# Attention products as 64x64 quarters of the array, with scores and values in one pair of banks

## The chip, the cores and the metric

The kernel runs on one core of a Trainium2 chip. The core has a matrix engine (TensorE, in the profile PE, with its weight loads as PEld), VectorE (DVE), ScalarE (ACT), GpSimd (POOL) and a queue engine (SP, SyncE) that issues the transfers here. Each engine works through a fixed list of instructions in order; semaphores make one wait for another. The metric is the time of one execution on the device in microseconds (us), lower is better.

## The reference

Two parts follow each other: attention within chunks of 64 tokens, then a feed-forward layer with a rational activation.

```
q, k, v: (8, 8, 576, 64)                       # batch, heads, tokens, head width; 9 chunks of 64 tokens
scores = matmul(q_c, k_c^T) / 8                # 64x64 for each chunk and head
attn = exp(scores - max); attn = attn / (sum(attn) + 1e-9)
x = matmul(attn, v_c)                          # back to (4608 tokens, 512)
h = x @ w_in                                   # (512, 2048)
P = a0 + a1*h + a2*h^2 + a3*h^3;  Q = 1 + |b0||h| + |b1|h^2
out = (P / (Q + 1e-6)) @ w_out                 # (2048, 512)
```

## The kernel before

The 4608 tokens are 36 units of 128 tokens: a unit is two chunks of 64 tokens with all eight heads. Three units make a block of 384 tokens, so there are 12 blocks. A block's feed-forward part has 8 steps, each over 256 of the 2048 inner columns.

**Feed-forward.** Each factor of the two large products is split into a high and a low part in the fp32r format, and three of the four partial products are summed. A step's first product is `ff1_mm`: 24 matmuls with 384 columns (line 252) into the tile `ph`, two banks of PSUM, of which there is one buffer. ScalarE copies it to `h` (line 281, one buffer too), then forms A, B and C (lines 282 to 284), a logarithm and an exponential (lines 288 and 289); VectorE makes `ghi` and `glo` of these (lines 293 to 306). The second product, `ff2_mm`, has 18 matmuls of 512 columns (line 334) into the three banks `po`. It is written two steps behind the first one (LAG).

**Attention of a unit** runs ahead, in the steps of the block before. `att_s` (line 163) makes the scores. Queries, keys and values lie with the two chunks in the upper and lower 64 partitions, and head pair (`hp`), head of the pair and 64 columns along the free side. The keys are kept in a tile `kbd` of twice the width, in which each chunk's rows have their keys on their own side and zeros on the other; so one matmul with 128 rows, 64 stationary columns (one head) and 128 moving columns gives both chunks' scores without mixing them. There are 8 of these, and they write the lower or upper 64 partitions of a bank, by head. Then come VectorE's maximum (line 183), eight exponentials of 64 columns with their sums on ScalarE (line 187), and the division. `att_t` (line 200) transposes the result on TensorE into the bank `pst` and copies it in two halves into `abd`, zero-padded like `kbd`. `att_av` (line 212) multiplies with the values, again 8 matmuls of the same shape, into the bank `psx`; ScalarE copies to `xhi`, and VectorE makes `xlo`.

**Banks.** PSUM has 8 banks: two for `ph`, three for `po`, and one each for `pss` (scores), `pst` and `psx`. The first three units' scores use `po`. Zeros are written once: by GpSimd into `abd`, into `kbd`, and into early keys of units 1 and 2, which borrow other tiles.

**Weights** arrive as float64 in 32 pieces of 512 columns. `piece_decode` (line 118) rewrites each with three instructions of VectorE and two of ScalarE; the low part is made by VectorE, or, for the pieces in LO_ON_PE, by two matmuls (lines 130 and 131) into a tile `pl`, which takes one of `pss`, `pst`, `psx` in turn. Four raw buffers hold the pieces in flight. PROLOGUE gives the order at the start, DECODED the pieces that are due before each of the first ten steps.

**What sets the order.** The instructions of all engines come from a scheduler, which takes the written order as priority and its own estimate of times. So a piece of a product can be put between others, and the order of the main loop is a wish only. The last two steps are written out by hand.

Of the kernel before, what the change touches and what calls it, by code (L numbers as in the profile page):

```python
# [29 lines left out]
KLN = 32  # L30
EXP_WIDE = (0, 1)
XLO_ON_PE = ()
LO_ON_PE = (7, 10, 11, 12, 13, 14, 16, 17, 18, 19, 20, 21, 22, 23, 25, 29)
PROLOGUE = "L0 L1 l1 L2 p1 l2 S0 S1 l1 V0 T0 p1 A0 p1 T1 p1 S2 V1 V2 A1 L3 T2 A2"
DECODED = (10, 11, 12, 16, 18, 25, 26, 28, 31, 32)
# [3 lines left out]
def tile_chunked_attention_rational_moe(  # L39
# [11 lines left out]
    nc = tc.nc  # L51
# [7 lines left out]

# [1 line left out]
    wi_hi = cp.tile([P, NHP, DFF], F32R, tag="wi_hi", name="wi_hi")  # L61
# [33 lines left out]
    def zero_rest(kt):  # L95
        nc.gpsimd.memset(kt[0:64, 1, :], 0.0)
        nc.gpsimd.memset(kt[64:128, 0, :], 0.0)

    def load_early(u):
        flat = lambda t: t.rearrange("p a b -> p (a b)")  # L100
        kt = p2.tile([P, NHP, BT], F32, tag=("xhi", "xlo")[u % 2], name=f"kt{u}")
        kt = flat(kt)[:, :1024].rearrange("p (a b) -> p a b", a=2)
        qt = p2.tile([P, 2, BT], F32, tag="A", name=f"qt{u}")
        vt = p2.tile([P, 2, BT], F32, tag="B", name=f"vt{u}")
        zero_rest(kt)
        load(u, flat(qt)[:, :512], kt, flat(vt)[:, :512], "q")
# [11 lines left out]
    def piece_decode(i, hi, lo):  # L118
# [8 lines left out]
        if i in LO_ON_PE:  # L127
            tag = ("pss", "pst", "psx")[i % 3]
            pl = ps_a.tile([P, 512], F32, tag=tag, name="pl")
            nc.tensor.matmul(pl, ident, val, start=True, stop=False)  # L130
# [28 lines left out]

# [1 line left out]
    ebuf = {}  # L161

    def att_s(u):
        qt, kt, vt = loaded[u]
        if u < UPB:
            pss = ps_o.tile([P, 512], F32, tag=f"po{u}", name=f"pss{u}")
        else:
            pss = ps_a.tile([P, 512], F32, tag="pss", name=f"pss{u}")
        for hp in range(NHP):
            for j in range(2):  # L170
                c0 = hp * 128 + j * 64
                nc.tensor.matmul(  # L172
                    pss[j * 64:(j + 1) * 64, hp * 128:(hp + 1) * 128],
                    qt[:, c0:c0 + 64],
                    kt[:, :, c0:c0 + 64],
                    start=True, stop=True,
                )
        g3 = pss.rearrange("p (g k) -> p g k", k=64)
        st = p2.tile([P, 4, 8], F32, tag="sm", name=f"sm{u}")
        mx, nm, sm, rs = (st[:, i, :] for i in range(4))  # L180
        e = p2.tile([P, 512], F32, tag="e", name=f"e{u}")
        e3 = e.rearrange("p (g k) -> p g k", k=64)
        nc.vector.tensor_reduce(mx, g3, AX.X, ALU.max)
        if EXP_ACCUM[u % 3] and u not in EXP_WIDE:
            nc.vector.tensor_scalar_mul(nm, mx, -0.125)
            for g in range(8):
                nc.scalar.activation(  # L187
                    e3[:, g, :], g3[:, g, :], AF.Exp,
                    bias=nm[:, g:g + 1], scale=0.125, accum_out=sm[:, g:g + 1],
                )  # L190
        else:
            nc.vector.tensor_sub(e3, g3, mx.unsqueeze(2).to_broadcast([P, 8, 64]))
            nc.scalar.activation(e, e, AF.Exp, scale=0.125)
            nc.vector.tensor_reduce(sm, e3, AX.X, ALU.add)
        nc.vector.tensor_scalar_add(rs, sm, 1e-9)
        nc.vector.reciprocal(rs, rs)
        nc.vector.tensor_mul(e3, e3, rs.unsqueeze(2).to_broadcast([P, 8, 64]))
        ebuf[u] = e

    def att_t(u):  # L200
        e = ebuf.pop(u)
        pst = ps_a.tile([P, 512], F32, tag="pst", name=f"pst{u}")
        for hp in range(NHP):
            c = slice(hp * 128, (hp + 1) * 128)
            nc.tensor.transpose(pst[:, c], e[:, c], ident)  # L205
        for par in range(2):
            rows = slice(64 * par, 64 * par + 64)
            nc.scalar.copy(abd[rows, par, :], pst[rows, :])

    xbuf = {}  # L210

    def att_av(u):
# [7 lines left out]
        qt, kt, vt = loaded.pop(u)  # L220
        psx = ps_a.tile([P, NHP, 128], F32, tag="psx", name=f"psx{u}")
        on_pe = u in XLO_ON_PE
        for hp in range(NHP):
            for j in range(2):
                c0 = hp * 128 + j * 64
                nc.tensor.matmul(  # L226
                    psx[j * 64:(j + 1) * 64, hp, :],
                    vt[:, c0:c0 + 64],
                    abd[:, :, c0:c0 + 64],
                    start=True, stop=not on_pe,  # L230
                )
        tk = slice(i * 128, (i + 1) * 128)
        nc.scalar.copy(xhi[:, :, tk], psx)
        if on_pe:
            nc.tensor.matmul(psx, nident, xhi[:, :, tk], start=False, stop=True)
            nc.scalar.copy(xlo[:, :, tk], psx)
        else:
            nc.vector.tensor_sub(xlo[:, :, tk], psx, xhi[:, :, tk].bitcast(F32))  # L238

# [1 line left out]
    gbuf = {}  # L241
# [112 lines left out]

# [1 line left out]
    win = lambda fq: [w_in_piece(fq, cc) for cc in range(NHP)]  # L356
# [29 lines left out]

# [1 line left out]
    total = RUN_NB * NST  # L388
    for g in range(total - 2):
# [8 lines left out]
        if n + 1 < RUN_NB and s % 2 == 0:  # L398
            if 0 < s // 2 <= UPB:
                att_av(u - 1)  # L400
                load(u)
            if s // 2 < UPB:
                att_s(u)
        if g >= LAG:
            n2, s2 = divmod(g - LAG, NST)
            ff2_mm(n2, s2)
            if s2 == NST - 1:
                store(n2)
        if n + 1 < RUN_NB and s % 2 == 1 and s // 2 < UPB:
            att_t(u)  # L410

# [1 line left out]
    with tc.manual_schedule():  # L413
# [57 lines left out]
```

## Time and profile before

| what | us |
|---|---|
| time, median of 3 runs (lowest to highest) | 972.9 (972.42 to 973.03) |
| the profiled execution, from its first to its last instruction | 971.9 |
| L252, first matrix: three groups of 760 matmuls, 260.0 + 256.9 + 256.6 | 773.5 |
| L334, second matrix: three groups of 570 matmuls, 227.3 + 222.8 + 150.4 | 600.5 |
| L172, scores: 544 + 32 records, 50.2 + 3.9 | 54.1 |
| L226, values: 576 records | 43.0 |
| L205, transposes: 144 | 22.8 |
| L187, exponentials: 272 of 128x64, mean 323 ns, with sums read behind each, mean 216 ns | 82.0 + 58.8 |
| L208, copies into abd: 72 of 64x512, mean 583 ns | 41.9 |

The times of groups add up to more than the engine's busy time, since a matmul's record goes on after the next one has begun. The profile names a group by line, engine, operation and tiles. Its chain of work that ended last follows back from the last instruction what each waited for. Its windows give busy times for chosen stretches, its timeline the instructions in order, where x16 is a number of records. The profiler lists no other time of the profiled execution than the span; the granted clock of TensorE was 0.993 on average.

### The profile page before, as it was taken

What the parts mean: (1) busy time and instruction counts of PE and PEld (TensorE: products, weight loads), DVE (VectorE), ACT (ScalarE), POOL (GpSimd) and SP (SyncE); (2) the same over time, 40 slices, a digit from 0 to 9 for tenths busy, and PEclk for the clock granted to TensorE, in tenths of its full rate; (3) what the DMA queues carried; (4) which work ended last, traced back from release to release, by engine and by line L of the source; (5) the groups of instructions that cost most, each with busy time, mean ns of one, the idle gap of its engine ahead of it and who ended that gap; (6) DMA issues with size and microseconds to landing.
All of it is one profiled execution on the core that took longest, in us unless ns stands there. A gap on an engine that the chain in (4) does not pass through costs nothing.

```text
span 971.9 us, 14009 instructions
## 1 busy us (share of the span) xinstructions
PE 942.6 (97%) x5376; PEld 816.3 (84%) x5376; DVE 787.5 (81%) x1011; ACT 702.0 (72%) x1353; POOL 4.9 (1%) x16
## 2 busy tenths in 40 slices
PE   4599999999999999999999999999999999999998
PEld 3477788898888888888888888888888888888996
DVE  6799999878787887887887887877877878877786
ACT  4799889758667777667767767775876776775764
POOL 2000000000000000000000000000000000000000
PEclk9799999999999999999999999999999999999999
DMA  7644423002002112101101100110111211100000
GB/s 252 189 154 142 163 87 110 12 1 66 4 30 66 33 33 65 34 12 59 61 12 52 56 24 26 62 44 23 65 33 34 65 33 34 65 12 1 33 1 33
DMA packets 26274, 55.43 MB, mean 57 GB/s; under 512 B 3680, under 2 KB 3680, under 8 KB 26208
## 3 DMA queue, kind: packets, MB, share of 16 engines
q1 hardware_dynamic: 26208, 54.54, 17.7%
q8 instruction: 42, 0.69, 0.3%
q14 instruction: 24, 0.20, 0.1%
HBM read 45.09 MB, written 9.44 MB: 56 GB/s over the span
## 4 chain that ended last, share of the span: by engine, by line
PE 89%; DVE 4%; DMA 3%; ACT 3%; issue 1%; SPq 1%; DVEq 0%; ACTq 0%
PE po L334 40%; PE ph L252 39%; PE pss L172 4%; PE psx L226 3%; DMA raw<-in_w_in 2%; PE pst L205 1%; DMA raw<-in_w_out 1%; PE pl L130 1%; ACT e L187 1%; DVE raw L124 1%; ACT raw L123 0%; DVE raw L125 0%; DVE raw L122 0%; SPq L90 0%; DVE C L295 0%
## 5 line engine op out<-in xcount | busy, mean ns | idle before, releaser
L252 PE MATMUL ph<-xhi,wi_hi 128*128 128x384 f32 x760 | 260.0, 342 | 3.7 <-ACT h L281 3.0
L252 PE MATMUL ph<-xlo,wi_hi 128*128 128x384 f32 x760 | 256.9, 338 | 0.2 <-DVE xlo L238 0.2
L252 PE MATMUL ph<-xhi,wi_lo 128*128 128x384 f32 x760 | 256.6, 338 | 0.0
L334 PE MATMUL po<-wo_hi,ghi 128*128 128x512 f32 x570 | 227.3, 404 | 0.0
L334 PE MATMUL po<-wo_lo,ghi 128*128 128x512 f32 x570 | 222.8, 396 | 0.0
L281 ACT COPY h<-ph 128x768 f32<-128x768 f32 x95 | 76.1, 802 | 202.1 <-PE ph L252 199.3
L252 PEld LDWEIGHTS ph<-xhi,wi_hi 128*128 128x128 f32 x760 | 143.3, 189 | 14.1 <-ACT h L281 4.4
L293 DVE SCALAR_TENSOR_TENSOR B<-B,ab,A 128x768 f32<-128x768 f32 x95 | 96.6, 1017 | 67.7 <-ACT B L283 67.1
L334 PE MATMUL po<-wo_hi,glo 128*128 128x512 f32 x570 | 150.4, 397 | 0.0
L252 PEld LDWEIGHTS ph<-xlo,wi_hi 128*128 128x128 f32 x760 | 143.4, 189 | 3.9 <-DVE xlo L238 0.7
L252 PEld LDWEIGHTS ph<-xhi,wi_lo 128*128 128x128 f32 x760 | 143.4, 189 | 0.8 <-issue 0.5
L334 PEld LDWEIGHTS po<-wo_hi,ghi 128*128 128x128 f32 x570 | 107.0, 188 | 27.0 <-issue 5.3
L303 DVE SCALAR_TENSOR_TENSOR ghi<-C,ab,A 128x768 fp32r<-128x768 f32 x94 | 95.7, 1018 | 41.7 <-ACT A L289 35.6
L334 PEld LDWEIGHTS po<-wo_hi,glo 128*128 128x128 f32 x570 | 106.7, 188 | 26.3 <-issue 0.8
L334 PEld LDWEIGHTS po<-wo_lo,ghi 128*128 128x128 f32 x570 | 107.0, 188 | 21.5 <-issue 1.6
L288 ACT ACTIVATE A<-B,cst 128x768 f32<-128x768 f32 x95 | 89.6, 943 | 13.4 <-DVE B L293 13.0
L305 DVE SCALAR_TENSOR_TENSOR B<-C,ab,B 128x768 f32<-128x768 f32 x95 | 96.8, 1019 | 2.5
L295 DVE SCALAR_TENSOR_TENSOR C<-C,ab,h 128x768 f32<-128x768 f32 x95 | 96.6, 1017 | 1.9
L284 ACT ACTIVATE C<-h,ab 128x768 f32<-128x768 f32 x95 | 96.6, 1017 | 0.1
L306 DVE TENSOR_TENSOR glo<-B,A 128x768 fp32r<-128x768 f32 x94 | 89.9, 956 | 5.4
L294 DVE TENSOR_TENSOR C<-C,h 128x768 f32<-128x768 f32 x95 | 90.4, 952 | 3.8 <-ACT C L284 3.8
L304 DVE SCALAR_TENSOR_TENSOR B<-B,ghi 128x768 f32<-128x768 f32 x94 | 90.0, 957 | 2.5
(95 smaller groups left out, 993.4 us busy)
## 6 DMA issues: line engine op xcount, KB each, us to landing
qt<-in_qT SPq DMA_DIRECT2D x36, 256.0 KB, 2.9
vt<-in_vP SPq DMA_DIRECT2D x36, 256.0 KB, 2.8
out<-o SPq DMA_DIRECT2D x36, 256.0 KB, 2.2
kbd<-in_kT SPq DMA_DIRECT2D x68, 128.0 KB, 3.3
raw<-in_w_in SPq DMA_DIRECT2D x16, 512.0 KB, 4.8
raw<-in_w_out SPq DMA_DIRECT2D x16, 512.0 KB, 3.7
kt<-in_kT SPq DMA_DIRECT2D x4, 128.0 KB, 4.7
ab<-in_a SPq DMA_DIRECT2D x1, 2.0 KB, 2.5
```

Source lines behind the costliest of these rows:

```text
L252: nc.tensor.matmul(acc, w, x[:, cc, :], start=(k == 0), stop=(k == 11))
L281: yield nc.scalar.copy(h, ph[:, :, :BT])
L284: yield nc.scalar.activation(C, h, AF.Identity, bias=a2, scale=a3)
L288: nc.scalar.activation(A, B, AF.Ln, bias=cst[:, 0:1], scale=2.0 ** -KLN)
L293: yield nc.vector.scalar_tensor_tensor(B, B, b1a, A, ALU.mult, ALU.add)
L294: yield nc.vector.tensor_mul(C, C, h)
L295: yield nc.vector.scalar_tensor_tensor(C, C, a1, h, ALU.add, ALU.mult)
L303: yield nc.vector.scalar_tensor_tensor(ghi, C, a0, A, ALU.add, ALU.mult)
L304: yield nc.vector.scalar_tensor_tensor(B, B, CQ, ghi.bitcast(F32), ALU.add, ALU.mult)
L305: yield nc.vector.scalar_tensor_tensor(B, C, a0, B, ALU.add, ALU.subtract)
L306: yield nc.vector.tensor_mul(glo, B, A)
L334: nc.tensor.matmul(obuf[n][i], g[:, fi, i * 128:(i + 1) * 128], w[:, 2 * s + fi, :], start=(s == 0 and k == first[i]), stop=(s == NST - 1 ...
```

## The change

The keys are no longer padded: `kt` is an ordinary tile, loaded by one transfer. `quarters` makes a product of 16 matmuls with 64 rows (one chunk), 64 stationary columns (one head) and 64 moving columns; the rows come from chunk `c`, the output partitions from head `par`, and chunk `c` writes bank `c` of a two-bank tile. The built program marks each with a tile of 64x64 at one of four places in the array. `att_t` copies once into `at`. Scores and values share one tile `pq` of two banks; the values of units 0 to 2 and the scores of unit 1 use `ph` instead. `pl` takes `po` for pieces below PL_EARLY, later `pst` for odd and half of `pq` for even pieces. The main loop writes `att_s` behind `ff2_mm`, where it stood ahead of it. The last step's first product takes `pq`.

```
+PL_EARLY = 12
...
-            qt = p2.tile([P, 512], F32, tag="qt", name=f"qt{u}", bufs=1)
-            vt = p2.tile([P, 512], F32, tag="vt", name=f"vt{u}", bufs=1)
-            kt = kbd
+            qt, kt, vt = (p2.tile([P, 512], F32, tag=t, name=f"{t}{u}", bufs=1) for t in ("qt", "kt", "vt"))
...
-        for par in range(2):
-            rows = slice(64 * par, 64 * par + 64)
-            nc.sync.dma_start(out=kt[rows, par, :], in_=kT[u, rows, :])
+        nc.sync.dma_start(out=kt, in_=kT[u])
...
-            tag = ("pss", "pst", "psx")[i % 3]
-            pl = ps_a.tile([P, 512], F32, tag=tag, name="pl")
+            if i < PL_EARLY:
+                pl = ps_o.tile([P, 512], F32, tag=f"po{i % 3}", name="pl")
+            elif i % 2:
+                pl = ps_a.tile([P, 512], F32, tag="pst", name="pl")
+            else:
+                pl = ps_a.tile([P, 2, 512], F32, tag="pq", name="pl")[:, 0, :]
...
+    def pair(early, name):
+        pool, tag = (ps_h, "ph") if early else (ps_a, "pq")
+        return pool.tile([P, 2, 512], F32, tag=tag, name=name)
+
+    def quarters(out, stat, mov):
+        for hp in range(NHP):
+            for par in range(2):
+                for c in range(2):
+                    rows = slice(64 * c, 64 * c + 64)
+                    cols = slice(hp * 128 + par * 64, hp * 128 + par * 64 + 64)
+                    nc.tensor.matmul(
+                        out[par * 64:(par + 1) * 64, c, hp * 64:(hp + 1) * 64],
+                        stat[rows, cols], mov[rows, cols], start=True, stop=True,
+                    )
 
     def att_s(u):
         qt, kt, vt = loaded[u]
-        if u < UPB:
-            pss = ps_o.tile([P, 512], F32, tag=f"po{u}", name=f"pss{u}")
-        else:
-            pss = ps_a.tile([P, 512], F32, tag="pss", name=f"pss{u}")
-        for hp in range(NHP):
-            for j in range(2):
-                c0 = hp * 128 + j * 64
-                nc.tensor.matmul(
-                    pss[j * 64:(j + 1) * 64, hp * 128:(hp + 1) * 128],
-                    qt[:, c0:c0 + 64],
-                    kt[:, :, c0:c0 + 64],
-                    start=True, stop=True,
-                )
+        pss = pair(u == 1, f"pss{u}")
+        quarters(pss, qt, kt)
...
-        for par in range(2):
-            rows = slice(64 * par, 64 * par + 64)
-            nc.scalar.copy(abd[rows, par, :], pst[rows, :])
+        at = p2.tile([P, 512], F32, tag="at", name=f"at{u}")
+        nc.scalar.copy(at, pst)
+        abuf[u] = at
...
-        psx = ps_a.tile([P, NHP, 128], F32, tag="psx", name=f"psx{u}")
...
+        psx = pair(u < UPB, f"psx{u}")
+        quarters(psx, vt, abuf.pop(u))
...
-            if s // 2 < UPB:
-                att_s(u)
         if g >= LAG:
             n2, s2 = divmod(g - LAG, NST)
             ff2_mm(n2, s2)
             if s2 == NST - 1:
                 store(n2)
-        if n + 1 < RUN_NB and s % 2 == 1 and s // 2 < UPB:
-            att_t(u)
+        if n + 1 < RUN_NB and s // 2 < UPB:
+            (att_t if s % 2 else att_s)(u)
```

How the rows of the engines moved is shown at three places. The line numbers of the change are its own (234 for 252, 316 for 334, 162 for 172 and 226, 263 for 281, 119 and 120 for 130 and 131). In a name, `ph5_0` is block 5, step 0, `po4_0` the first bank of block 4, `ghi4_7` the step 7 whose values are read, `pss18` the scores of unit 18.

First TensorE at the start of block 5. Before, with the first rows of step 0 left out:

```order
L252 MATMUL ph5_0_3764<-xhi5_3318,wi_lo_72 128x384
L172 MATMUL pss18_3808<-kbd_76,qt18_3678 64x128 x5
L334 MATMUL po4_0_3361<-wo_hi_73,ghi4_6_3735 128x512
...
L334 MATMUL po4_0_3361<-wo_lo_74,ghi4_7_3797 128x512
L252 MATMUL ph5_1_3850<-xhi5_3318,wi_hi_71 128x384
...
L252 MATMUL ph5_1_3850<-xhi5_3318,wi_lo_72 128x384
L334 MATMUL po4_1_3362<-wo_hi_73,ghi4_7_3797 128x512
...
L172 MATMUL pss19_3991<-kbd_76,qt19_3985 64x128 x2
L252 MATMUL ph5_2_3928<-xhi5_3318,wi_hi_71 128x384
```

The same place in the change, from the last values of the block to the first matmul of step 2:

```order
L162 MATMUL psx17_3935<-at17_3889,vt17_3768 64x64 x16
L316 MATMUL po4_0_3581<-wo_hi_73,ghi4_7_4073 128x512
...
L316 MATMUL po4_2_3583<-wo_hi_73,glo4_7_4074 128x512 x2
L234 MATMUL ph5_0_4040<-xlo5_3555,wi_hi_71 128x384
...
L234 MATMUL ph5_0_4040<-xhi5_3554,wi_lo_72 128x384
L162 MATMUL pss18_4102<-kt18_3955,qt18_3954 64x64 x16
L234 MATMUL ph5_1_4134<-xhi5_3554,wi_hi_71 128x384
...
L234 MATMUL ph5_1_4134<-xhi5_3554,wi_lo_72 128x384
L234 MATMUL ph5_2_4212<-xhi5_3554,wi_hi_71 128x384
```

Before, second-matrix rows of steps 6 and 7 stand between the steps 0, 1 and 2 of the next block. In the change they all stand ahead of step 0, whose operands need the values product `psx17`; only the whole scores product is left between steps 0 and 1, and nothing between steps 1 and 2.

Second, ScalarE at the same place. Before:

```order
L281 COPY h5_0_3789<-ph5_0_3764 128x768
L282 ACTIVATE A5_0_3790<-h5_0_3789,ab_78 128x768
L283 ACTIVATE B5_0_3791<-h5_0_3789 128x768
L284 ACTIVATE C5_0_3792<-h5_0_3789,ab_78 128x768
L187 ACTIVATE e18_3818,sm18_3817<-pss18_3808,sm18_3817 128x64 x7
L288 ACTIVATE A5_0_3790<-B5_0_3791,cst_90 128x768
L187 ACTIVATE e18_3818,sm18_3817<-pss18_3808,sm18_3817 128x64
L289 ACTIVATE A5_0_3790<-A5_0_3790,cst_90 128x768
L281 COPY h5_1_3875<-ph5_1_3850 128x768
```

And in the change:

```order
L263 COPY h5_0_4065<-ph5_0_4040 128x768
L264 ACTIVATE A5_0_4066<-h5_0_4065,ab_76 128x768
L265 ACTIVATE B5_0_4067<-h5_0_4065 128x768
L266 ACTIVATE C5_0_4068<-h5_0_4065,ab_76 128x768
L182 ACTIVATE e18_4120,sm18_4119<-pss18_4102,sm18_4119 128x64 x7
L270 ACTIVATE A5_0_4066<-B5_0_4067,cst_86 128x768
L182 ACTIVATE e18_4120,sm18_4119<-pss18_4102,sm18_4119 128x64
L263 COPY h5_1_4159<-ph5_1_4134 128x768
L271 ACTIVATE A5_0_4066<-A5_0_4066,cst_86 128x768
```

The rows are the same but for the last two, which changed places: the copy of step 1 now stands ahead of step 0's last exponential.

Third, TensorE in block 0 around the weight pieces, whose numbers are those of `raw`. Before, in steps 5 and 6:

```order
L131 MATMUL pl_848<-wi_hi_71,nident_83 128x512
...
L130 MATMUL pl_857<-raw22_810,ident_75 128x512
L131 MATMUL pl_857<-wi_hi_71,nident_83 128x512
L252 MATMUL ph0_6_956<-xhi0_180,wi_hi_71 128x384
...
L172 MATMUL pss6_1184<-kbd_76,qt6_1011 64x128 x2
L130 MATMUL pl_866<-raw23_812,ident_75 128x512
L172 MATMUL pss6_1184<-kbd_76,qt6_1011 64x128 x6
```

And in the change, around the beginning of step 6:

```order
L162 MATMUL pss5_846<-kt5_823,qt5_822 64x64 x16
L119 MATMUL pl_924<-raw21_884,ident_75 128x512
L234 MATMUL ph0_6_1032<-xhi0_184,wi_hi_71 128x384
L234 MATMUL ph0_6_1032<-xlo0_185,wi_hi_71 128x384
L120 MATMUL pl_924<-wi_hi_71,nident_81 128x512
L119 MATMUL pl_897<-raw18_878,ident_75 128x512
L120 MATMUL pl_897<-wo_hi_73,nident_81 128x512
L119 MATMUL pl_915<-raw20_882,ident_75 128x512
L120 MATMUL pl_915<-wi_hi_71,nident_81 128x512
```

Pieces 18 and 20, which stood ahead of these places before, now stand behind the scores of unit 5; being even, they use a half of `pq`, where these scores lie, and they stand ahead of the rest of step 6.

More of the change, by code (lines that the diff above doesn't have):

```diff
@@ L31 @@
 EXP_WIDE = (0, 1)
-XLO_ON_PE = ()
 LO_ON_PE = (7, 10, 11, 12, 13, 14, 16, 17, 18, 19, 20, 21, 22, 23, 25, 29)
+PL_EARLY = 12
 PROLOGUE = "L0 L1 l1 L2 p1 l2 S0 S1 l1 V0 T0 p1 A0 p1 T1 p1 S2 V1 V2 A1 L3 T2 A2"
@@ L65, in tile_chunked_attention_rational_moe @@
     ident = cp.tile([P, P], F32, tag="ident", name="ident")
-    kbd = cp.tile([P, 2, 512], F32, tag="kbd", name="kbd")
-    abd = cp.tile([P, 2, 512], F32, tag="abd", name="abd")
     ab = cp.tile([P, 8], F32, tag="ab", name="ab")
@@ L87, in load_qk @@
         nc.sync.dma_start(out=qt, in_=qT[u])
-        for par in range(2):
-            rows = slice(64 * par, 64 * par + 64)
-            nc.sync.dma_start(out=kt[rows, par, :], in_=kT[u, rows, :])
+        nc.sync.dma_start(out=kt, in_=kT[u])
     def load_v(u):
         nc.sync.dma_start(out=loaded[u][2], in_=vP[u])
-    def zero_rest(kt):
-        nc.gpsimd.memset(kt[0:64, 1, :], 0.0)
-        nc.gpsimd.memset(kt[64:128, 0, :], 0.0)
     def load_early(u):
[L100 to L106, printed above, removed]
+        t = lambda tag, name: p2.tile([P, 2, BT], F32, tag=tag, name=name).rearrange("p a b -> p (a b)")[:, :512]
+        load(u, t("A", f"qt{u}"), t("C", f"kt{u}"), t("B", f"vt{u}"), "q")
     raws = {}
@@ L146, in tile_chunked_attention_rational_moe @@
     nc.vector.tensor_scalar_mul(nident, ident, -256.0)
-    nc.gpsimd.memset(abd[0:64, 1, :], 0.0)
-    nc.gpsimd.memset(abd[64:128, 0, :], 0.0)
     nc.sync.dma_start(out=ab[:, 0:4], in_=a.partition_broadcast(P))
@@ L157, in tile_chunked_attention_rational_moe @@
     nc.gpsimd.memset(cst[:, 1:2], -KLN * math.log(2.0))
-    ebuf = {}
+    ebuf, abuf = {}, {}
+    def pair(early, name):
[11 more added lines that the diff above has]
+                    )
@@ L178, in att_s @@
[L178 to L183, printed above, removed]
+        pss = pair(u == 1, f"pss{u}")
+        quarters(pss, qt, kt)
+        sc = pss[:, :, 0:256].rearrange("p c (h k) -> p c h k", k=64)
+        st = p2.tile([P, 4, 2, NHP], F32, tag="sm", name=f"sm{u}")
@@ L184, in att_s @@
+        mx, nm, sm, rs = (st[:, i] for i in range(4))
+        e = p2.tile([P, NHP, 2, 64], F32, tag="e", name=f"e{u}")
+        ec = e.rearrange("p h c k -> p c h k")
+        spread = lambda x: x.unsqueeze(3).to_broadcast([P, 2, NHP, 64])
+        nc.vector.tensor_reduce(mx, sc, AX.X, ALU.max)
         if EXP_ACCUM[u % 3] and u not in EXP_WIDE:
             nc.vector.tensor_scalar_mul(nm, mx, -0.125)
[L186 to L190, printed above, removed]
+            for c in range(2):
+                for hp in range(NHP):
+                    nc.scalar.activation(
+                        ec[:, c, hp, :], sc[:, c, hp, :], AF.Exp,
+                        bias=nm[:, c, hp:hp + 1], scale=0.125, accum_out=sm[:, c, hp:hp + 1],
+                    )
@@ L191, in att_s @@
         else:
-            nc.vector.tensor_sub(e3, g3, mx.unsqueeze(2).to_broadcast([P, 8, 64]))
+            nc.vector.tensor_sub(ec, sc, spread(mx))
             nc.scalar.activation(e, e, AF.Exp, scale=0.125)
-            nc.vector.tensor_reduce(sm, e3, AX.X, ALU.add)
+            nc.vector.tensor_reduce(sm, ec, AX.X, ALU.add)
         nc.vector.tensor_scalar_add(rs, sm, 1e-9)
         nc.vector.reciprocal(rs, rs)
-        nc.vector.tensor_mul(e3, e3, rs.unsqueeze(2).to_broadcast([P, 8, 64]))
+        nc.vector.tensor_mul(ec, ec, spread(rs))
@@ L203, in att_t @@
         for hp in range(NHP):
-            c = slice(hp * 128, (hp + 1) * 128)
-            nc.tensor.transpose(pst[:, c], e[:, c], ident)
-        for par in range(2):
-            rows = slice(64 * par, 64 * par + 64)
-            nc.scalar.copy(abd[rows, par, :], pst[rows, :])
+            nc.tensor.transpose(pst[:, hp * 128:(hp + 1) * 128], e[:, hp, :, :].rearrange("p c k -> p (c k)"), ident)
+        at = p2.tile([P, 512], F32, tag="at", name=f"at{u}")
+        nc.scalar.copy(at, pst)
+        abuf[u] = at
     xbuf = {}
@@ L220, in att_av @@
         qt, kt, vt = loaded.pop(u)
-        psx = ps_a.tile([P, NHP, 128], F32, tag="psx", name=f"psx{u}")
[L222 to L238, printed above, removed]
+        psx = pair(u < UPB, f"psx{u}")
+        quarters(psx, vt, abuf.pop(u))
+        x = psx[:, :, 0:256].rearrange("p c (h t) -> p c h t", t=64)
+        hi, lo = (y[:, :, i * 128:(i + 1) * 128].rearrange("p h (c t) -> p c h t", c=2) for y in (xhi, xlo))
+        nc.scalar.copy(hi, x)
+        nc.vector.tensor_sub(lo, x, hi.bitcast(F32))
     gbuf = {}
@@ L261, in ff1_mm_halves @@
     def ff1_mm_halves(n, s):
-        ph = [ps_a.tile([P, 1, 512], F32, tag=t, name=f"ph{t}") for t in ("pss", "pst")]
+        ph = ps_a.tile([P, 2, 512], F32, tag="pq", name="ph_end")
         for fi in range(2):
-            ff1_half(n, s, fi, ph[fi][:, 0, :BT])
-        return ph
+            ff1_half(n, s, fi, ph[:, fi, :BT])
+        return ph[:, 0:1, :], ph[:, 1:2, :]
     chain = {}
@@ L375, in first_load @@
         if u == 0:
-            zero_rest(kbd)
             load(0, part="q")
```

## The prediction

> **What bounds the kernel now.** I read the page's busy shares first, then the chain of work that ended last, the windows of the three stages, and the waits.
>
> ```profile
> span 971.9 us, 14009 instructions
> PE 942.6 (97%) x5376; PEld 816.3 (84%) x5376; DVE 787.5 (81%) x1011; ACT 702.0 (72%) x1353; POOL 4.9 (1%) x16
> PE 89%; DVE 4%; DMA 3%; ACT 3%; issue 1%; SPq 1%; DVEq 0%; ACTq 0%
> 0.00:45.00 45.00, 23.50 (x167) 19.09 (x167) 30.94 (x67) 27.59 (x82) 4.88 (x16) 0.89 0.74 234
> 45.00:140.00 95.00, 91.13 (x486) 73.00 (x487) 91.42 (x143) 84.01 (x164) 0.00 (x0) 0.98 0.42 136
> 200.00:900.00 700.00, 700.00 (x4020) 612.23 (x4019) 557.69 (x670) 498.82 (x952) 0.00 (x0) 1.00 0.12 38
> ACT h L281 <- PE ph L252: 199.3, 77, 4.1
> SPq L115 <- PE pl L130: 38.8, 13, 6.9
> ```
>
> The columns of the windows are stretch, length, busy time (count) of PE, PEld, DVE, ACT and POOL, granted clock, DMA share and GB/s. From 200 to 900 us TensorE is busy for all of 700.00 us: whatever leaves its queue there shortens the kernel, and whatever makes it wait lengthens it. Before 45 us it is idle for 21.5 us, and until 140 us VectorE (91.42 of 95.00 us) is as full as TensorE (91.13). ScalarE waits 199.3 us for the first matrix's product: it follows TensorE and has room on average. The queue on SP holds weight loads back for 38.8 us until TensorE has read the weight buffer before.
>
> **Products.** In this timeline (start, length) one values product stands whole between second-matrix matmuls, and five of the eight matmuls of a scores product stand between `ph` and `po`:
>
> ```profile
> 498.11 0.40 PE L334 MATMUL po<-wo_lo,ghi 128*128 128x512 f32 x1
> 498.44 0.85 PEld L226 LDWEIGHTS psx<-abd,vt 128*64 128x64 f32 x16 [0.37 <-issue]
> 498.44 1.09 PE L226 MATMUL psx<-abd,vt 128*64 128x128 f32 x16
> 499.46 0.50 PE L334 MATMUL po<-wo_hi,ghi 128*128 128x512 f32 x1
> 499.80 0.39 PE L334 MATMUL po<-wo_lo,ghi 128*128 128x512 f32 x1
> 439.69 0.34 PE L252 MATMUL ph<-xhi,wi_lo 128*128 128x384 f32 x1
> 439.95 0.87 PE L172 MATMUL pss<-kbd,qt 128*64 128x128 f32 x10
> 440.75 0.50 PE L334 MATMUL po<-wo_hi,ghi 128*128 128x512 f32 x1
> 441.09 0.39 PE L334 MATMUL po<-wo_lo,ghi 128*128 128x512 f32 x1
> 194.05 4.17 PE ph L252 x24
> 233.76 4.20 PE po L334 x18
> 492.82 0.60 PE L205 MATMUL pst<-ident,e 128*128 128x128 f32 x4
> L205 PE MATMUL pst<-ident,e x144: 270/272/448, 16.9 to 874.5; 128*128 128x128 f32 x144
> ```
>
> Each fp32 matmul of the program leaves two records (8 give x16), two passes. A `ph` matmul takes a slot of 4.17/24 = 0.174 us, a `po` 4.20/18 = 0.233. Without the product, the `po` of 499.80 would have started two slots after 498.11, at 498.58: the product cost 1.22 us. The piece of five cost 441.09 - 439.69 - 0.174 - 0.233 = 0.99. Eight matmuls make four pairs, one for each column half; if five count as three, the difference of one pair is 0.23 us and what is left for entering and leaving the smaller shape is about 0.35; I take 0.22 a pair, since 4 x 0.22 + 0.35 = 1.23. So a pass of 128 columns takes 0.11. Four transposes start within 0.60 - 0.27 = 0.33 us, again 0.11 for 128 columns, on the full array: a half needs no longer per pass than the whole, and the two halves run side by side.
>
> A product now is 16 matmuls in four groups of four quarters, two passes of 64 columns: if all four run side by side, 4 x 2 x 0.055 = 0.44 us, with 0.35 around it 0.79. No row shows a quarter, so I bound it. It can't fall under 0.44, since the four quarters then fill the array at the pace of a full pass. If only column halves run side by side it is 8 x 2 x 0.055 = 0.88, as before. If nothing does, 32 x 0.055 = 1.76. I take 0.44: the nearest row, the column halves, shows parts of the array that work at the same time.
>
> The printed order of before has 576 of these matmuls in 83 pieces, 36 of them odd: 306 pairs x 0.22 + 83 x 0.35 = 96.4 us. The new one has 72 pieces: 72 x 0.79 = 56.9. **First term: -39.5 us.**
>
> [...] The trace has 16 loads in 0.85 us, which fits loads in a row as well as loads that merely follow the pairs, so it can't decide; this is the third rival below.
>
> **The new order.** With one pair of banks (`pq`) for scores and values, the values of a block's last unit come later, behind `po` of step 6 (the first two fences of the section on the change). Then `ph` of steps 0, 1 and 2 stand with only a scores product and nothing between them; `ph` has one buffer, so each waits for ScalarE's copy `h` of the one before. ScalarE's rows at such a start, and a restart of TensorE behind a copy:
>
> ```profile
> 440.06 0.80 ACT L281 COPY h<-ph 128x768 f32<-128x768 f32 x1 [3.63 <-PE ph L252]
> ...
> 443.39 0.29 ACT L187 ACTIVATE e<-pss,sm 128x64 f32<-128x64 f32 x1
> ...
> 445.42 0.96 ACT L288 ACTIVATE A<-B,cst 128x768 f32<-128x768 f32 x1
> 446.24 0.34 ACT L187 ACTIVATE e<-pss,sm 128x64 f32<-128x64 f32 x1
> 446.44 0.23 ACT L187 ACTIVATION_READ_ACCUMULATOR e<-pss,sm 128x1 f32 x1
> 446.53 0.96 ACT L289 ACTIVATE A<-A,cst 128x768 f32<-128x768 f32 x1
> 46.13 0.78 ACT L281 COPY h<-ph 128x768 f32<-128x768 f32 x1
> 46.96 0.69 PE L252 MATMUL ph<-xhi,wi_hi 128*128 128x384 f32 x1 [2.55 <-ACT h L281]
> ```
>
> The change has the same rows up to 446.53, and there the next copy `h` stands in place of L289. So copy follows copy after 446.53 - 440.06 = 6.47 us. TensorE restarts 0.83 us after a copy's start, and its first matmul is drawn out by 0.11 (0.50 against 0.39 behind the product above). Step 1 starts 0.94 us after the first copy begins, needs 4.17 and could hand over at 5.11; step 2 starts at 6.47 + 0.94 = 7.41. That wait is 2.3 us. Between steps 0 and 1 the pause is 1.1 us (a matmul's 0.34 less its slot of 0.17, then 0.94), and the product there covers all but some 0.3. Counting row by row with the gaps between instructions I get 3.0 a block; the two bounds are 2.3 and 3.3. Blocks 2 to 10 have it; the last block has the two pauses without a product, 2.5. **Second term: 9 x 3.0 + 2.5 = +29.5 us.** Behind the waiting matmuls stand all others of the queue; DVE and ACT then wait for PE. What hid this before is the `po` of steps 6 and 7, 4.2 us each, and these now stand ahead of step 0.
>
> **Start.** Scores hold `pq` until their last exponential: 439.95 to 446.53 above, 6.6 us. In the third pair of order fences the split of weight piece 18 wants `pq` right behind the scores of unit 5, with some 1.3 us of other rows between: a wait of about 5 us in TensorE's queue, and SP's next load waits for that split (the 38.8 us above). Other such places are shorter. Counting all printed rows of the first 200 us forward, each at its engine's end or its operands', whichever is later, with the intervals above, I get 17 us more of TensorE waiting than in the order of before counted alike, 6 of them ahead of 45 us, where S0 and S2 share `pq`. From below, VectorE alone already fills 45 to 140 us, so the products' gain there (12 x 0.5) can't show: +6. From above, doubling what I can't place gives 24. **Third term: +17 us.**
>
> **At nothing:** one 128-partition copy of the transposed weights for two of 64 rows (36 fewer on ScalarE, hidden by its 199.3 us of waiting; were it the bound, they would be a gain); eight memsets fewer on GpSimd (4.9 us in all, ahead of the first product, which waits for the loads too); one keys transfer for two (DMA share 0.12). The strided views have as many elements.
>
> **Sum:** -39.5 + 29.5 + 17 = +7. The span of 971.9 becomes 979; the median of the runs, 972.9, lies 1.0 above the profiled span, so **980 us**. [...]
>
> **Rivals.** *The start is cheap.* If VectorE's decoding, not the shared bank, sets the first 140 us, the third term is +6, the sum -4, the time 969: faster. For it: 91.42 of 95.00 us. Against: the bank is held for 6.6 us, and 38.8 us of loads already wait for TensorE. It decides when the start costs under 8 us (sum below -2). 0.14. *Row halves don't run side by side:* each product costs 0.44 more, but some fourteen stand where TensorE waits anyway: 58 x 0.44 = +25, 1005. For it: no row shows row quarters together. 0.14. *Loads or issue in a row,* or quarters not formed at all: 32 x 0.053 (0.85/16) = 1.7 a product, +1.26 x 72 = +91, 1071. 0.06.
>
> **How the numbers follow.** The forecast has 0.66 with its own range of 972 to 988, from block waits of 2.3 to 3.3 (9 x 0.5 = 5) and a start of 9 to 24. A measurement of this kernel tells 0.2%, 2 us, from no change. Of the forecast's 0.66, 0.59 is slower, 0.05 the same, 0.02 faster; of the cheap start 0.11 faster and 0.03 the same; the others are slower. That gives 0.13, 0.08, 0.79. The range from 970 to 1006 leaves out the dear loads, half of the cheap start and a little of the row halves.
>
> **What would show it.** A product of 32 records in about 0.8 us, with the matmul behind it, confirms the first term; 1.2 the second rival, 2 the third. Idle time of PE ahead of `ph`, released by ACT `h`, of some 30 us in all from 200 us on, twice a block, confirms the second; with none the sum is far off. PE's idle time in the first 200 us tells the third: 25 us now, 40 by my count, 30 if the start is cheap. If ScalarE's exponentials were quicker, or the waits fell where the queue had other work, the prediction would be too slow.

## The result and the profile after

The changed kernel takes **983.6 us** (median of four runs, 981.9 to 986.3) against 973.0 (972.4 to 973.5): a ratio of 1.0106, interval 1.0086 to 1.0126. It is slower by 10.7 us. The first fence has, from the page of the changed kernel, its span, TensorE's busy row and the chain, then three windows and four rows of the waits (us in total, times, longest). This execution took 986.26 us, 2.6 over the median.

```profile
span 984.5 us, 16171 instructions
PE 922.2 (94%) x6528; PEld 797.8 (81%) x6528; DVE 787.0 (80%) x1011; ACT 685.3 (70%) x1317; POOL 0.8 (0%) x8
PE 84%; ACT 8%; DVE 4%; DMA 2%; issue 1%; SPq 0%; ACTq 0%
...
0.00:45.00 45.00, 18.05 (x253) 13.69 (x254) 32.85 (x68) 24.69 (x65) 0.77 (x8) 1.00 0.67 225
45.00:140.00 95.00, 86.09 (x508) 66.31 (x507) 83.66 (x128) 76.62 (x139) 0.00 (x0) 0.93 0.41 130
200.00:900.00 700.00, 679.20 (x4946) 596.44 (x4946) 554.27 (x681) 490.84 (x971) 0.00 (x0) 0.99 0.14 42
...
ACT h L263 <- PE ph L234: 83.3, 49, 2.8
PEld ph L234 <- ACT h L263: 31.7, 24, 2.4
PE ph L234 <- ACT h L263: 24.7, 22, 2.0
PE pl L119 <- ACT e L182: 5.4, 1, 5.4
```

TensorE does less work (922.2 us for 942.6) in a longer span. From 200 to 900 us it was never idle before; now it lacks 700 - 679.20 = 20.8 us. ScalarE's share of the chain went from 3% to 8%. TensorE's waits for ScalarE's copy `h` grew from 3.0 us to 24.7, and one wait of 5.4 us is new: the split `pl` waits for the exponentials `e`. In turn ScalarE waits for TensorE only 83.3 us where it was 199.3. In the first 140 us TensorE is idle for 26.95 + 8.91 = 35.9 us against 25.4. The granted clock of 1.00 in the first window is not a reading: the trace has no clock before 44.4 us, and the rows show half clock until then (see the third term below).

A values product in TensorE's timeline (start, length, operation):

```profile
472.33 0.40 PE L316 MATMUL po<-wo_lo,ghi 128*128 128x512 f32 x1
472.65 0.69 PE L162 MATMUL psx<-at,vt 64*64 64x64 f32 x32
473.28 0.97 PE L316 MATMUL po<-wo_hi,glo 128*128 128x512 f32 x3
```

The 32 records take 0.69 us, where 16 took 1.09. The slot as the prediction counts it: 473.28 - 472.33 = 0.95, less a `po` slot of 0.233, is 0.72; the `po` behind is drawn out by about 0.1, so 0.82 in all. The single records of this product start in groups of four, 7 ns apart within a group, and the next group 58 ns later. All four quarters run together.

Three block starts in time order, the wait in brackets: of the first and the last only step 2, of the middle one the scores product, step 1 and step 2:

```profile
387.69 0.44 PE L234 MATMUL ph<-xhi,wi_hi 128*128 128x384 f32 x1 [2.04 <-ACT h L263]
...
457.61 0.69 PE L162 MATMUL pss<-kt,qt 64*64 64x64 f32 x32
458.56 0.45 PE L234 MATMUL ph<-xhi,wi_hi 128*128 128x384 f32 x1 [0.26 <-ACT h L263]
465.05 0.44 PE L234 MATMUL ph<-xhi,wi_hi 128*128 128x384 f32 x1 [2.05 <-ACT h L263]
...
540.85 0.44 PE L234 MATMUL ph<-xhi,wi_hi 128*128 128x384 f32 x1 [2.04 <-ACT h L263]
```

TensorE pauses 0.26 us ahead of step 1 and 2.05 ahead of step 2, in each of the nine block starts of this stretch: 9 x 2.31 = 20.8, all of its idle time there. The rows also measure blocks. From 465.05 to 540.85 is 75.80 us; from 387.69 to 465.05 it is 77.36, with the same waits. The extra 1.56 us is a matter of the clock:

```profile
387.00:393.00 6.00, 5.31 (x21) 5.30 (x22) 5.51 (x8) 5.42 (x7) 0.00 (x0) 0.72 0.01 3
464.00:470.00 6.00, 4.95 (x30) 4.87 (x31) 5.16 (x8) 5.46 (x10) 0.00 (x0) 1.00 0.00 0
```

In these windows of the changed kernel the granted clock (third number from the right) was 0.72 behind the wait of 387.69 and 1.00 behind that of 465.05. A mean of 0.72 over 6 us is 3.4 us at half clock. In this execution four of the nine waits of 2.05 us were followed by such a stretch, begun 0.9 to 1.5 us after the wait ended.

### The profile page after: what moved, and what is told of

Read it like the earlier page. It is cut to its first block, busy times and chain, and to the rows that moved or that the text cites. A ratio compares the mean times of both kernels' runs of the same rounds, so it can differ in the third digit from the quotient of the medians.

```text
span 984.5 us, 16171 instructions
## 1 busy us (share of the span) xinstructions
PE 922.2 (94%) x6528; PEld 797.8 (81%) x6528; DVE 787.0 (80%) x1011; ACT 685.3 (70%) x1317; POOL 0.8 (0%) x8
## 4 chain that ended last, share of the span: by engine, by line
PE 84%; ACT 8%; DVE 4%; DMA 2%; issue 1%; SPq 0%; ACTq 0%
PE po L316 41%; PE ph L234 36%; ACT e L182 2%; PE psx L162 2%; ACT h L263 2%; DMA raw<-in_w_in 2%; PE pst L199 1%; PE pss L162 1%; PE pl L119 1%; ACT C L266 1%; ACT B L265 1%; ACT A L264 1%; DMA raw<-in_w_out 1%; DVE raw L110 1%; DVE raw L109 1%
## 5 line engine op out<-in xcount | busy, mean ns | idle before, releaser
L234 PE MATMUL ph<-xhi,wi_hi 128*128 128x384 f32 x760 | 264.7, 348 | 25.1 <-ACT h L263 24.7
L234 PE MATMUL ph<-xhi,wi_lo 128*128 128x384 f32 x760 | 260.5, 343 | 0.0
L316 PE MATMUL po<-wo_lo,ghi 128*128 128x512 f32 x570 | 225.1, 398 | 0.0
L234 PEld LDWEIGHTS ph<-xhi,wi_hi 128*128 128x128 f32 x760 | 145.9, 192 | 36.8 <-ACT h L263 31.7
L316 PE MATMUL po<-wo_hi,glo 128*128 128x512 f32 x570 | 154.3, 401 | 0.1
L263 ACT COPY h<-ph 128x768 f32<-128x768 f32 x95 | 76.5, 806 | 111.7 <-PE ph L234 83.3
L234 PEld LDWEIGHTS ph<-xlo,wi_hi 128*128 128x128 f32 x760 | 146.0, 192 | 2.9 <-issue 0.3
L234 PEld LDWEIGHTS ph<-xhi,wi_lo 128*128 128x128 f32 x760 | 145.8, 192 | 1.6 <-issue 1.3
L316 PEld LDWEIGHTS po<-wo_hi,ghi 128*128 128x128 f32 x570 | 107.4, 189 | 22.9
L316 PEld LDWEIGHTS po<-wo_hi,glo 128*128 128x128 f32 x570 | 104.7, 188 | 24.6 <-DVE glo L288 0.8
L277 DVE SCALAR_TENSOR_TENSOR C<-C,ab,h 128x768 f32<-128x768 f32 x95 | 96.4, 1015 | 1.6
L271 ACT ACTIVATE A<-A,cst 128x768 f32<-128x768 f32 x95 | 89.9, 946 | 2.3
```

The source lines that it names most:

```text
L234: nc.tensor.matmul(acc, w, x[:, cc, :], start=(k == 0), stop=(k == 11))
L263: yield nc.scalar.copy(h, ph[:, :, :BT])
L271: nc.scalar.activation(A, A, AF.Exp, bias=cst[:, 1:2], scale=-1.0)
L277: yield nc.vector.scalar_tensor_tensor(C, C, a1, h, ALU.add, ALU.mult)
L316: nc.tensor.matmul(obuf[n][i], g[:, fi, i * 128:(i + 1) * 128], w[:, 2 * s + fi, :], start=(s == 0 and k == first[i]), stop=(s == NST - 1 ...
```

## The experiments

Seven kernels ran; their times stand beside 983.6 (the change) and 973.5 to 973.6 (before, run again beside them).

**x1_shift: attention one step earlier.** Each unit's load, scores, transposes and values are written one step earlier, so that the last values of a block no longer come last.

```diff
-        u = (n + 1) * UPB + s // 2
-        if n + 1 < RUN_NB and s % 2 == 0:
-            if 0 < s // 2 <= UPB:
+        ahead = [divmod(k, NST) for k in ((0, 1) if g == 0 else (g + 1,))]
+        for m, q in ahead:
+            u = (m + 1) * UPB + q // 2
+            if m + 1 < RUN_NB and q % 2 == 0 and 0 < q // 2 <= UPB:
                 att_av(u - 1)
                 load(u)
...
-        if n + 1 < RUN_NB and s // 2 < UPB:
-            (att_t if s % 2 else att_s)(u)
+        for m, q in ahead:
+            u = (m + 1) * UPB + q // 2
+            if m + 1 < RUN_NB and q // 2 < UPB:
+                (att_t if q % 2 else att_s)(u)
```

> The change, with each unit's attention written one step earlier. Theory (the waits at each block's start come from the last values of the block being late, so that no second-matrix matmul is left between steps 0, 1 and 2): the waits of PE for the copy h fall from 56.4 us in all (31.7 and 24.7 for PEld and PE) to under 8, PE is idle for under 3 us between 200 and 900 us (20.8 in the change), and the time falls by 25 to 32 us, to 952 to 959. Rival (sharing the pair of banks costs the time wherever the rows stand): waits of the same size come back at another row, time 978 to 986. Rival (the quarters themselves cost the time): 978 to 986 with no waits.

Measured 953.3 (952.8 to 954.2), ratio to before 0.9794, interval 0.9777 to 0.9812. Its span, the window of the steady blocks, the waits for the first matrix and two copies `h` of step 5, one block apart:

```profile
span 952.4 us, 16177 instructions
...
200.00:900.00 700.00, 700.00 (x5100) 618.32 (x5099) 578.91 (x702) 506.05 (x983) 0.00 (x0) 1.00 0.13 42
...
ACT h L263 <- PE ph L234: 106.0, 57, 4.4
PE ph L234 <- ACT h L263: 2.4, 1, 2.4
...
411.63 0.80 ACT L263 COPY h<-ph 128x768 f32<-128x768 f32 x1 [3.36 <-PE ph L234]
484.78 0.80 ACT L263 COPY h<-ph 128x768 f32<-128x768 f32 x1 [1.14 <-PE ph L234]
```

TensorE is busy for all of the 700 us again, the block-start waits are gone (24.7 us to 2.4) and ScalarE waits for TensorE instead. The quarters and the shared banks are as in the change; only the place of the work moved. So the waits come from where the last values stand, and are worth 30 us together with the half clock behind them. A block now takes 484.78 - 411.63 = 73.15 us. The kernel before, in the same two steps:

```profile
412.55 0.80 ACT L281 COPY h<-ph 128x768 f32<-128x768 f32 x1 [1.90 <-PE ph L252]
488.82 0.80 ACT L281 COPY h<-ph 128x768 f32<-128x768 f32 x1 [2.31 <-PE ph L252]
```

76.27 us. In both kernels TensorE is full throughout, so the difference, 3.12 us for six products, is the bare gain of the quarters: 0.52 us a product.

**x2_chunk_outer: the same quarters in another order.** The loop over row halves goes outside.

```diff
-        for hp in range(NHP):
-            for par in range(2):
-                for c in range(2):
+        for c in range(2):
+            for hp in range(NHP):
+                for par in range(2):
```

> The change, with the loop over chunks outermost in each product, so that neighbouring matmuls are two column halves of the same rows and the lower rows' quarters come last. Theory (matmuls start in the order of the program, and a quarter that is busy holds up what stands behind it, so only two quarters work at a time): a product costs 1.2 to 1.3 us instead of 0.82 and the time rises by 12 to 22 us, to 996 to 1006. Rival (the engine picks free quarters out of its queue): product 0.8 and 980 to 987.

Measured 1004.7 (1001.5 to 1004.9), ratio to before 1.0317, interval 1.0295 to 1.0338: 21 us over the change. A product, and the waits of two block starts:

```profile
453.68 0.97 PE L162 MATMUL psx<-at,vt 64*64 64x64 f32 x32
...
785.52 0.44 PE L234 MATMUL ph<-xhi,wi_hi 128*128 128x384 f32 x1 [2.05 <-ACT h L263]
862.70 0.44 PE L234 MATMUL ph<-xhi,wi_hi 128*128 128x384 f32 x1 [2.05 <-ACT h L263]
```

The product takes 0.97 us for 0.69. Its single records start in 13 groups 58 ns apart where the change has 8: ten groups of two, and three of four in the middle, where the second row half begins beside the end of the first. Five groups more are 0.29 us. So a product costs 1.10 us; the expectation had 1.2 to 1.3, for it had no such overlap in the middle. The longer product hides the pause of 0.26 us at the block start, so a block without a half-clock stretch is 862.70 - 785.52 - 75.80 = 1.4 us longer, six times 0.28 less 0.26. In this execution eight of the nine waits were followed by half clock, which is most of the rest of the 21 us. That the time lies in the expected range is therefore partly luck: the product grew less than expected, and the clock made up for it. So of these two orders the row halves run side by side throughout only in the one whose quarters alternate between them (8 groups in 0.69 us, against 13 in 0.97).

**x3_written_order: only the text as before.** The scores are written ahead of the second matrix again, with quarters and shared banks kept.

```diff
                 att_av(u - 1)
                 load(u)
+            if s // 2 < UPB:
+                att_s(u)
...
-        if n + 1 < RUN_NB and s // 2 < UPB:
-            (att_t if s % 2 else att_s)(u)
+        if n + 1 < RUN_NB and s % 2 == 1 and s // 2 < UPB:
+            att_t(u)
```

> The change, with the main loop written as before the change: scores ahead of the second matrix, transposes behind it. Theory (the shared banks, not the place in the text, delay the last values of a block): waits at the block starts stay, 976 to 983. Rival (the new place of the scores in the text made the values late): the waits go, 950 to 960.

Measured 979.6 (978.2 to 984.2), ratio to before 1.0079, interval 1.0049 to 1.0108. The steady window and the wait:

```profile
200.00:900.00 700.00, 681.49 (x4945) 598.36 (x4945) 559.84 (x684) 492.31 (x968) 0.00 (x0) 1.00 0.13 41
...
PE ph L234 <- ACT h L263: 23.2, 20, 2.1
```

The waits are still there, so the place in the text does not delay the last values. That leaves the one pair of banks, and TensorE's order fits it: before, the next unit's scores have begun (549.4 us) when a unit's values start (555.2), and with the pair, here as in the change, scores start only behind the values ahead of them (values at 493.5, scores at 499.9). Quarters with banks of their own were not run, so this cause is argued by elimination. The runs overlap those of the change (981.9 to 986.3), and this execution had two half-clock stretches behind block starts for four.

**x4_pl_pst: splits out of the shared banks.** From piece 12 on all splits write to `pst`.

```diff
-            elif i % 2:
-                pl = ps_a.tile([P, 512], F32, tag="pst", name="pl")
             else:
-                pl = ps_a.tile([P, 2, 512], F32, tag="pq", name="pl")[:, 0, :]
+                pl = ps_a.tile([P, 512], F32, tag="pst", name="pl")
```

> The change, with the splits of weight pieces from 12 on all in the bank of the transposes, none in the pair of scores and values. Theory (in the first 200 us the splits wait for the scores' exponentials in the shared pair): the wait of PEld for ACT e at the splits (5.7 us) goes and the time falls by 2 to 6 us, to 978 to 982. Rival (decoding on VectorE sets the start, the bank does not matter): no change within 1.5 us of the change.

Measured 980.0 (979.5 to 980.5), ratio to before 1.0071, interval 1.0055 to 1.0087. First the place of the wait in the change, with its window; then the same for x4_pl_pst, whose lines stand two lower:

```profile
107.58 1.22 PE L119 MATMUL pl<-raw,ident 128*128 128x512 f32 x1 [5.37 <-ACT e L182]
...
100.00:120.00 20.00, 13.93 (x32) 7.52 (x33) 16.57 (x27) 14.13 (x34) 0.00 (x0) 0.74 0.43 134
```

```profile
107.83 1.17 PE L117 MATMUL pl<-raw,ident 128*128 128x512 f32 x2 [1.32 <-ACT wi_lo L119]
111.22 1.17 PE L117 MATMUL pl<-raw,ident 128*128 128x512 f32 x2 [1.46 <-ACT wi_lo L119]
114.21 1.17 PE L117 MATMUL pl<-raw,ident 128*128 128x512 f32 x2 [1.07 <-ACT wi_lo L119]
117.23 0.44 PE L232 MATMUL ph<-xhi,wi_lo 128*128 128x384 f32 x1 [1.10 <-ACT wi_lo L119]
...
100.00:120.00 20.00, 15.04 (x56) 9.98 (x57) 17.64 (x31) 13.38 (x35) 0.00 (x0) 1.00 0.54 168
45.00:140.00 95.00, 84.80 (x527) 66.67 (x526) 86.82 (x132) 78.28 (x141) 0.00 (x0) 1.00 0.39 130
```

The wait of 5.37 us is gone, and four others of together 4.95 us stand in its place, for ScalarE's part of the decoding. TensorE's idle time from 45 to 140 us does not fall (10.2 us for 8.9). What falls is the half clock: 0.74 over 20 us is some 10 us of it, and with x4_pl_pst it is 1.00. TensorE worked in 7.8 of these 10 us and waited in the others, so this stretch cost 3.9 us. A second stretch is gone with it, 3.4 us behind a wait at 56 us, another 1.7 us; that wait is there in x4_pl_pst too (2.0 us for 1.7), so this part is chance. The span is 977.8 against 984.5: 3.9 + 1.7, and 1.6 from three late stretches instead of four, less 1.3 of idle time. So the wait for the bank cost through the clock, and its own length covered waits that were due anyway.

**x5_shift_start: x1_shift with a mended start.** The edit of x4_pl_pst on top of x1_shift, and other points of decoding. The expectation calls them later, but the numbers are the pieces due before each step: two more are due before steps 2, 4 and 7, and one fewer before step 5, so most of it is earlier.

```diff
-DECODED = (10, 11, 12, 16, 18, 25, 26, 28, 31, 32)
+DECODED = (10, 11, 14, 16, 20, 24, 26, 30, 31, 32)
```

> The shifted kernel x1_shift (953.3 us) with two edits to its start: from piece 12 on all splits on TensorE write to pst, and the pieces are decoded a little later (DECODED 10, 11, 14, 16, 20, 24, 26, 30, 31, 32). Theory (what is left of the start's loss is the splits' wait for banks that the scores' exponentials hold): TensorE sits idle some 4 us less in the first 140 us, so 949 us, 947 to 952. Rival (the start is set by the pieces' loads and their decoding on VectorE and ScalarE): 953 or more, and TensorE idle as long as in x1_shift.

Measured **947.5** (945.8 to 949.0), ratio to before 0.9732, interval 0.9712 to 0.9752, which beats both kernels. Its span and the first two windows, then those of x1_shift:

```profile
span 943.6 us, 16179 instructions
...
0.00:45.00 45.00, 18.92 (x257) 14.55 (x258) 33.43 (x70) 25.19 (x66) 0.77 (x8) 1.00 0.67 230
45.00:140.00 95.00, 87.64 (x566) 68.45 (x565) 88.74 (x136) 80.88 (x158) 0.00 (x0) 1.00 0.41 133
```

```profile
0.00:45.00 45.00, 17.98 (x252) 13.62 (x253) 31.90 (x67) 24.78 (x65) 0.77 (x8) 1.00 0.65 223
45.00:140.00 95.00, 83.99 (x521) 65.59 (x520) 83.27 (x126) 74.31 (x135) 0.00 (x0) 0.95 0.41 131
```

Idle time of the first 140 us falls from 38.0 to 33.4, 4.6 us where the theory gave some 4, and the clock from 45 to 140 us rises from 0.95 to 1.00, worth up to 4.8 us in these executions. Which of the two edits brought the idle time down was not tried apart.

**x6_twice: each product issued twice on x1_shift.** The second time overwrites the first; the work is doubled and the result is the same.

```diff
-        for hp in range(NHP):
+        for hp in [k for _ in range(2) for k in range(NHP)]:
```

> x1_shift with each product's 32 quarters issued twice, the second over the first, so that the result is unchanged. It prices a product by itself. The profile of after shows single starts of quarters four at a time, the fours 58 ns apart: eight fours are 0.46 us, and what is above that in the 0.82 us of a product is entering and leaving the small tiles. If the first term's price is right and TensorE bounds the kernel, 66 to 72 products of 0.46 to 0.52 us more give 953.3 + 30 to 37 = 983 to 991. Rival (quarters run beside the neighbouring matmuls, so they cost nearly nothing): 953 to 960. Rival (each four costs what a product of 0.82 us costs over 8 fours): 953.3 + 72 x 0.82 = 1012.

Measured 993.5 (992.5 to 994.3), ratio to before 1.0205, interval 1.0185 to 1.0225. A product, two copies `h` a block apart, and the start's window:

```profile
444.04 1.16 PE L162 MATMUL psx<-at,vt 64*64 64x64 f32 x64
...
434.18 0.80 ACT L263 COPY h<-ph 128x768 f32<-128x768 f32 x1 [1.04 <-PE ph L234]
510.12 0.80 ACT L263 COPY h<-ph 128x768 f32<-128x768 f32 x1 [1.05 <-PE ph L234]
...
45.00:140.00 95.00, 83.39 (x654) 64.97 (x650) 75.63 (x115) 69.01 (x139) 0.00 (x0) 0.88 0.36 117
```

A block takes 75.94 us, 2.79 more than x1_shift, 0.465 for each product: eight groups of 58 ns. The record grows by the same, 1.16 - 0.69 = 0.47. So a product is 0.47 us of passes and 0.35 around them. Twelve blocks of 2.79 are 33.5 of the 40.2 us; the rest lies in the start, with 2.3 us more of idle time in the first 140 us and a clock of 0.88 for 0.95 from 45 to 140 us. The time came out 2.5 us over what was expected.

**x7_again: work put into the wait.** In the changed kernel, the first half of step 1's `ph` is computed twice in each block start, 12 x 0.173 = 2.08 us of work that changes nothing else.

```diff
             ff1_half(n, s, fi, ph[:, fi, :BT])
+            if n and s == 1 and fi == 0:
+                ff1_half(n, s, fi, ph[:, fi, :BT])
```

> The changed kernel (983.6 us) with twelve more matmuls of L234 in step 1 of blocks 1 to 9: the first half of ph is computed twice, the second time over the first. That is 12 x 0.173 = 2.08 us of work per block, 18.7 us in all, put where TensorE otherwise waits for ACT h. Theory (the block start is bound by the copy of h, and a stretch of half clock follows such a wait): the work lies in the wait and costs 0 to 6 us, the waits for ACT h fall from 55 to some 25 us, and there are fewer half-clock stretches behind block starts: 980 to 990. Rival (TensorE is what bounds at block starts too, the wait being made up elsewhere): 983.6 + 18.7 = 1002. On the clock alone: if the half-clock stretches come from the waits, at most two are left after 200 us; if they come whatever TensorE does, four as before.

Measured 986.0 (983.5 to 986.8), ratio to before 1.0124, interval 1.0103 to 1.0144. The steady window and the wait:

```profile
200.00:900.00 700.00, 693.52 (x5050) 612.47 (x5044) 558.00 (x683) 493.40 (x971) 0.00 (x0) 1.00 0.13 42
...
PE ph L234 <- ACT h L265: 5.2, 11, 2.0
```

18.7 us of added work cost 2.4 us of time, about what the runs of the two kernels scatter. The idle time of the window falls from 20.8 to 6.5 us, and no half-clock stretch is left in it. Two things hide in the 2.4 us. A block now takes 76.29 us, 0.49 more than a clean one of the change, for 2.08 us of work; and the four stretches of half clock that are gone gave back 6.2 us. So the work lies mostly in the wait: TensorE does not bound the block start; ScalarE's copy does. This kernel's printed order moved in places too (the second matrix of steps around the block start), so the clock's part rests on all kernels together, below.

## Why the prediction was right

The span grew by 984.5 - 971.9 = 12.6 us where +7 was predicted; the median grew by 10.7.

- **First term, -39.5: measured -37.4.** A product's slot is 0.82 us where 0.79 was predicted, and the gain is 3.12 us a block (0.52 x 6), 12 blocks if the first ones gain as much. By the prediction's count a product cost 96.4 / 72 = 1.34 us before, in its pieces, so 0.52 is what it should be. The two parts came out as argued: passes 0.47 (0.44), entering and leaving 0.35 (0.35). The rival of row halves that don't run together failed for this order of the quarters; x2_chunk_outer shows that it would have come true for another, at 0.28 us a product instead of 0.44. The rival of loads in a row gave 2 us a product and fell with the first record: 32 loads hide in 0.69 us. Its +91 us counted 32 loads one behind the other at 0.053 us (0.85/16, from the loads of before), which no run shows: a load's record is about as long as before (141 ns on average for a values product, against 143), but the 32 of this product overlap and are through in 0.56 us.
- **Second term, +29.5: measured about +32.** The two pauses of a block start were predicted as some 0.3 and 2.3 us and are 0.26 and 2.05, released by ACT `h`, as the prediction's reading of ScalarE's rows had it. A clean block is 75.80 - 73.15 = 2.65 us longer than x1_shift's, the pauses and the drawn-out restarts, against 3.0; nine of them are 23.9. The last block has 0.89 + 1.13 us:

```profile
916.46 0.45 PE L234 MATMUL ph<-xhi,wi_hi 128*128 128x384 f32 x1 [0.89 <-ACT h L263]
922.02 0.44 PE L234 MATMUL ph<-xhi,wi_hi 128*128 128x384 f32 x1 [1.13 <-ACT h L263]
```

  With 2.0 for it and 4 x 1.56 for the clock, which the prediction did not have, the sum is 32.1. Without the clock it is 25.9, 3.6 less than predicted: the mechanism was right, and that the size fits so well is partly luck. What x1_shift takes away, 984.5 - 952.4 = 32.1, is the same within the 2 us by which the two starts may differ in the clock.
- **Third term, +17: what is left is +18.** 12.6 + 37.4 - 32.1 = 17.9. Its size is right, its mechanism only in part, and the fit is partly luck. The wait of `pl` for the exponentials stands where it was predicted (5.4 us for about 5), but TensorE's idle time rose by 10.5 us, to 36, where 40 was counted and 30 would have been the cheap start. Of the 10.5, 5.5 lie ahead of 45 us, where the prediction had 6. Another 4.7 us are half clock, at which the prediction's sum had nothing. The trace has a clock from 22.9 us on before and from 44.4 us on in the change; until then the rows show half clock, as here in the change, where a `ph` matmul takes 0.32 us and then 0.17:

```profile
43.73 0.52 PE L234 MATMUL ph<-xhi,wi_lo 128*128 128x384 f32 x1
44.05 0.50 PE L234 MATMUL ph<-xhi,wi_hi 128*128 128x384 f32 x1
44.57 0.34 PE L234 MATMUL ph<-xhi,wi_lo 128*128 128x384 f32 x1
44.74 0.34 PE L234 MATMUL ph<-xhi,wi_hi 128*128 128x384 f32 x1
```

  So counted, TensorE worked for 28.7 us of the first 140 at half clock, where it was 19.3 before; half of the difference is 4.7 us (an estimate, since these first stretches are read from rows). The other 2.7 of the 17.9 are not placed. x4_pl_pst shows that without the wait of `pl` the decoding's own waits come in its place; what that wait cost was some 4 us at half clock. The cheap start needed less than +8 here and is refuted. The products' gain that cannot show in a start bound by loads and decoding (6 us in the prediction) was argued, not measured.
- **At nothing:** ScalarE's busy time fell from 702.0 to 685.3 us and GpSimd's from 4.9 to 0.8 without a trace in the sum, as said: neither stands on the chain where they were removed.

So the steady blocks gained 3.1 us each and lost 2.65 and a share of half clock, near zero; what made the kernel slower is mainly the start. The quarters were a good trade, paid for twice by the order that came with them. Moving the attention one step ahead gets the 32 us back.

## What to carry to other kernels

A saving on a full engine was worth its slots only while the queue behind it stayed full (3.12 us a block in x1_shift, of which the change lost 2.65 to its waits): before tiles are made to share a bank, look where the last of them will stand, and whether the work that used to cover a single-buffered tile still lies there. When small tiles of the array are packed, let row halves alternate in program order (0.82 us a product here, 1.10 in the other order). When a wait is named at one instruction, ask which wait is due next before pricing it at its length (in place of the 5.37 us here came others of together 4.95).

## What the runs showed of the hardware

**Short waits can cost twice.** At a TensorE wait the granted clock was sometimes halved for about 3.4 us or a small multiple (in the change 3.41 us from 389.14, 10.24 from 105.83). A wait of 2.05 us at a block start was followed by it in four of nine cases of the change, eight of nine of x2_chunk_outer, two of eight of x3_written_order and three of nine of x4_pl_pst, at some 1.6 us each. A wait of 4.5 to 5.4 us ahead of `pl` near 105 us brought 6.8 to 10.2 us of it, begun within the wait, in every one of the five kernels that have that wait (the change, x1_shift, x2_chunk_outer, x3_written_order, x7_again) and in neither of the two that don't and are otherwise close (x4_pl_pst, x5_shift_start). From 200 to 900 us no kernel without the waits of 2.05 us (before, x1_shift, x5_shift_start, x6_twice, x7_again) has a single such stretch.

**Which wait is punished depends on where it falls.** The stretches of one execution lie on a grid: in the change they begin at 235.54, 389.14, 617.83 and 846.53 us, which are 45, 67 and 67 steps of 3.413 us apart. Laid over the 35 waits of 2.05 us in the four kernels, this grid tells them apart: the 17 that have at least 1.89 us within one step were followed by half clock in the next step, and the 18 that are split, with at most 1.77 us in either, were not. So equal waits differ by luck, and a change of order moves that luck. Idle time within a step does not decide it alone: in the start, steps with 1.7 us of it were followed too (in the change the one from 54.63 us, with 1.72 us, by half clock from 58.05 to 61.46). The stretches also scatter the times: the four runs of the change have spans from 980.1 us at a mean clock of 0.991 to 984.5 at 0.985.

**Quarters cost by their order.** Four 64x64 quarters start 7 ns apart and the next four 58 ns later when row halves alternate; mostly two at a time, in 13 groups for 8, when they don't. Entering and leaving such a piece costs 0.35 us for the quarters (0.82 less the 0.47 that doubling adds), and about as much for the old shape by the prediction's working, so over two fifths of a product of 0.82 us is transition.
